# Output items of a fused attention and spectral kernel: the last 64 rows moved to the middle, the second half by batch

## The chip, the cores and the metric

The kernel runs on one core of one Trainium2 chip. Its time is the device time of one execution in microseconds (us); the median of several runs is the time of a kernel. A profile is of one execution, and gives the span from the first to the last thing that the profiler saw; the execution's own time is a little longer than its span.

## The reference

Eight batches, eight heads, 576 positions, head dimension 64. A sparse attention (heads 0 to 3 look back 31 positions, heads 4 to 7 look at earlier positions of the same residue modulo 32) gives `x` of 8 x 576 x 512. Then the lowest 64 Fourier modes along the positions are mixed by one complex 512 x 512 matrix each, transformed back to `y`, and the output is `u + relu(u @ w_ch)` with `u = x + y`:

```python
X = np.fft.rfft(x, axis=1)
Y[:, :n_modes] = Yr + 1j * Yi          # per mode: X[:, m] times (w_r[m] + i w_i[m])
y = np.fft.irfft(Y, n=S, axis=1)
u = x + y
return (u + np.maximum(u @ w_ch, 0.0)).astype(np.float32)
```

The output is 8 x 576 x 512 in float32, 9.4 MB. The weights `w_r` and `w_i` are 134 MB in float32, loaded once and converted to float16 on the way.

## The kernel before

Attention comes first, then the mixing of the modes, with the weight loads (issued by GpSimd, L182 to L190) running from the start to about 394 us. Beside the modes each batch is mixed ahead: `premix` leaves `v0s[b]` (x times w_ch) and `xos[b]` (x itself), each 128 partitions x 4 x 512 for the rows 0 to 511, and `v0h`, `xoh` for the last 64 rows of two batches together. `renew` adds to them what the first spectra give. The order of the instructions is written by hand: every engine runs its own in the order in which the program gives them.

What is left after the last weights is the **tail**, from L1044 on. The spectra of the last 16 modes are made (`spec_z` and the transposes of L1053) and kept as `zzs` (spectra times w_ch) and `yys` (spectra): `zzs[0]` and `yys[0]` hold batches 0 to 3, `zzs[1]` and `yys[1]` batches 4 to 7, in 32 partitions for each batch, so that batch b lies in partitions 32 * (b % 4) and up. `zzs[1]` is made later, from `spec_z(3, 1, held)` in the loop (L1068), while `yys[1]` is made with `yys[0]`.

The output is then made in 18 **items**, numbered k from 0 to LAST = 17. Each is 128 partitions x 2 x 512 float32, 512 KB. The rows of a batch are in five groups t: for t < 4, partition p of group t holds the row 256 * (t // 2) + 2p + t % 2, and t = 4 is the last 64 rows (512 to 575).

- Items 0 to 7 are the pairs of batches (0, 1) and (2, 3) in turn, for t = 0, 1, 2, 3; items 8 to 15 the pairs (4, 5) and (6, 7). Such an item goes out in one transfer on SP's queue (L1028), with rows of 2 KB in the output; item 0 in two pieces.
- Items 16 and 17 are t = 4 for batches 0 to 3 and 4 to 7. Partitions 0 to 63 hold the even batch of a pair, 64 to 127 the odd one. They go out in eight transfers of 64 partitions, 128 KB each (L1031): six on SP's queue, two on ScalarE's.

One item is made in these steps. `v_early(k)`: two matmuls with the identity put v0 into PSUM (L987). `new_rows(k, vps[k], zzs)`: two matmuls with 32 rows each add the last modes (L1001); those of a pair use two of the four groups of 32 rows of TensorE. `v_done(k)`: ScalarE's Relu (L1013) into `rl`. `u_early`, `new_rows(k, ups[k], yys)`: the same for u (L992, L1001). `u_done(k)`: VectorE adds PSUM and `rl` into `osb` (L1020), and SP issues the transfer. The loop over k (L1067) writes the v part of item k between the u parts of k - 1, so the matmuls of L1001 for two neighbouring items stand together: zz of item k, then yy of item k - 1. The pairs alternate so that these four use four different row groups.

`osb` has five buffers (tag "w" of the pool `pw`); `rl` has four; vps and ups turn over three PSUM tiles "p" and one "u".

Of the kernel before, what the change touches and what calls it, by code (L numbers as in the profile page):

```python
# [56 lines left out]
def kernel(  # L57
# [10 lines left out]
    nc = tc.nc  # L68
# [17 lines left out]
    def psum(kind, half=False, pair=False):  # L86
        if pair:
            return pss[kind].tile([128, 2, 512], FP, tag=kind, name=kind)
        if half:
            return pss[kind].tile([128, 1024], F16, tag=kind, name=kind)  # L90
        return pss[kind].tile([128, 512], FP, tag=kind, name=kind)
# [146 lines left out]
    def normalise(val, den, n, pieces, dst):  # L238
        rec = pin.tile([128, 8], FP, tag="rec", bufs=4, name="rec")
        nc.vector.reciprocal(out=rec[0:n, 0:pieces], in_=den)  # L240
        nc.vector.tensor_tensor(  # L241
            out=dst,
            in0=val.rearrange("p h (q c) -> p h c q", c=4),
            in1=rec[0:n, 0:pieces]
            .to_broadcast((n, pieces, 64))
            .rearrange("p h (q c) -> p h c q", c=4),
            op=AluOp.mult,
        )

    def act_copy(out, in_):  # L250
        nc.scalar.activation(out=out, in_=in_, func=ACTF.Copy)  # L251
# [445 lines left out]
    def out_cols(t):  # L697
        if t < 4:
            return ds(256 * (t % 2) + 128 * (t // 2), 128)
        return ds(512, 64)  # L700
# [32 lines left out]
    def spec_z(g, bq, zp):  # L733
        for e in range(4):
            lhs = YS["YT"][:, e, g, ds(8 * bq, 8), :].rearrange("p x m -> p (x m)")
            nc.tensor.matmul(
                zp, lhs, w_chs["n"][:, e, :], start=(e == 0), stop=(e == 3)
            )
# [130 lines left out]
    zzs = [ptr.tile([128, DM], F16, name=f"zz{i}") for i in range(B)]  # L869
    yys = [ptr.tile([128, DM], F16, name=f"yy{i}") for i in range(B)]  # L870
# [31 lines left out]
    A3 = cs["cFl"].rearrange("p a t m -> p (a t m)")[:, 0:S]  # L902
# [64 lines left out]
    for n, i in enumerate([3, 5, 7] + list(range(8, 21))):  # L967
        b, t = n // 2, n % 2 * 2
# [1 line left out]
        if n % 4 == 3:  # L970
            late.setdefault(i + (b == B - 1), []).append(lambda b=b: renew(b, (4,)))

    items = []
    for P0 in (0, 2):
        items += [((2 * P, 2 * P + 1), t) for t in range(4) for P in (P0, P0 + 1)]
    items += [(range(b, b + 4), 4) for b in (0, 4)]
    LAST = len(items) - 1
    vps, ups, rls, osbs = {}, {}, {}, {}

    def own(item, kept, half):  # L980
        bs, t = item
        return [kept[b][:, t] for b in bs] if t < 4 else [half[b // 2] for b in bs[::2]]

    def v_early(k):
        vps[k] = psum("p", pair=True)
        for j, r in enumerate(own(items[k], v0s, v0h)):
            nc.tensor.matmul(vps[k][:, j], idn, r, start=True, stop=False)  # L987

    def u_early(k):
        ups[k] = psum(("p", "u")[k % 2], pair=True)  # L990
        for j, r in enumerate(own(items[k], xos, xoh)):
            nc.tensor.matmul(ups[k][:, j], idn, r, start=True, stop=False)  # L992

    def new_rows(k, acc, spectra):
        bs, t = items[k]
        for j, b in enumerate(bs):
            q = ds(32 * (b % 4), 32)
            o, cols = acc[:, j % 2], out_cols(t)
            if t == 4:
                o = acc[ds(64 * (b % 2), 64), j // 2]  # L1000
            nc.tensor.matmul(  # L1001
                o, A3[q, cols], spectra[b // 4][q], start=False, stop=True
            )

    def pieces(k):
        return [slice(0, 1), slice(1, 2)] if k == 0 else [slice(0, 2)]

    def v_done(k):
        rl = ptr.tile([128, 2, 576], FP, tag=("xT", "rl")[k // 2 % 2], bufs=2, name="rl")
        rls[k] = rl[:, :, 0:DM]  # L1010
        vp = vps.pop(k)
        for j in pieces(k):
            nc.scalar.activation(out=rls[k][:, j], in_=vp[:, j], func=ACTF.Relu)  # L1013

    def u_done(k):
        bs, t = items[k]
        up, rl = ups.pop(k), rls.pop(k)
        osb = pw.tile([128, 2, DM], FP, tag="w", name="osb")
        for j in pieces(k):
            nc.vector.tensor_tensor(  # L1020
                out=osb[:, j], in0=up[:, j], in1=rl[:, j], op=AluOp.add
            )
            if t < 4:
                rows = out[:, ds(128 * (t - t % 2), 256), :].rearrange(
                    "b (p i) e -> p b i e", i=2
                )
                own_b = slice(bs[0] + j.start, bs[0] + j.stop)
                nc.sync.dma_start(rows[:, own_b, t % 2], osb[:, j])  # L1028
        if t == 4:
            for b in bs:  # L1030
                (nc.scalar if b % 2 and k == LAST else nc.sync).dma_start(  # L1031
                    out[b, ds(512, 64), :], osb[ds(64 * (b % 2), 64), b // 2 % 2, :]
                )

    flush()
# [9 lines left out]
    with tc.tile_pool(name="ps_s", bufs=1, space=PSUM) as pss["s"]:  # L1045
        zp = pss["s"].tile([128, 512], FP, name="zp")
        yp = pss["s"].tile([128, 2, 512], F16, name="yp")
        spec_z(3, 0, zp)
        act_copy(zzs[0], zp)
        for bq in range(2):  # L1050
            for e in range(4):
                lhs = YS["YT"][:, e, 3, ds(8 * bq, 8), :].rearrange("p x m -> p (x m)")
                nc.tensor.transpose(yp[:, bq, ds(128 * e, 128)], lhs, idn)  # L1053
        for bq in range(2):
            nc.vector.tensor_copy(out=yys[bq], in_=yp[:, bq])
    pss["u"] = pctx.enter_context(tc.tile_pool(name="ps_u", bufs=1, space=PSUM))

    for k in range(2):
        new_rows(k, vps[k], zzs)
    for k in range(2):  # L1060
        v_done(k)
    for k in range(2):
        if k:
            u_early(k)
        new_rows(k, ups[k], yys)
        u_done(k)
    for k in range(2, LAST + 2):  # L1067
        if k == 8:  # L1068
            held = psum("p", pair=True)[:, 0]
            spec_z(3, 1, held)  # L1070
            act_copy(zzs[1], held)
        if k <= LAST:
            v_early(k)
        if k > 2:
            u_early(k - 1)
        if k <= LAST:
            new_rows(k, vps[k], zzs)
        if k > 2:
            new_rows(k - 1, ups[k - 1], yys)
        if k <= LAST:  # L1080
            v_done(k)
        if k > 2:
            u_done(k - 1)
# [31 lines left out]
```

## Time and profile before

| what | value |
|---|---|
| median of 6 runs | 429.23 us (428.49 to 429.43) |
| the profiled execution's own time | 428.49 us |
| its span | 426.7 us |
| TensorE busy | 346.0 us (81%), 4167 matmuls |
| VectorE busy | 235.0 us (55%) |
| ScalarE busy | 218.5 us (51%) |
| GpSimd busy | 110.7 us (26%) |
| transfers issued by GpSimd (inputs, weights) | 81.28 MB, 96.3% of 16 engines' span |
| transfers issued by SP (output, two constants) | 9.39 MB, 6.1% |
| HBM read, written | 162.83 MB, 9.44 MB |

The transfers of item 0's two pieces are issued at 396.5 us, the last of all at 423.1 us. From issue to landing the 512 KB transfers take 3.4 us in the median and the 128 KB ones 2.5 to 2.6 us. In a row of the timeline stand start, length, engine, line, operation and its operands, and in brackets how long the engine had been idle and what released it. A share of the DMA is the mean busy share of the core's 16 DMA engines. A PE row covers several matmuls where it has a count, and their ends are modelled.

### The profile page before, as it was taken

The page shows a single profiled execution, that of the slowest core. Times are in us where ns is not written, and L with a number is a line of the kernel's source. Part 1 is how long each engine was busy: PE and PEld are TensorE (multiplying, and loading weights), DVE is VectorE, ACT ScalarE, POOL GpSimd, SP SyncE. Part 2 cuts the span into 40 slices and gives each one's busy share as a digit, 9 for nine tenths or more (in the row PEclk, how much of TensorE's full clock was granted, in tenths as well). Part 3 has the DMA queues.
Part 4 walks back from the last instruction along what each step waited for, and adds up shares of the span by engine and source line. Part 5 has one row for each costly group of instructions (what it writes and reads, how often), then busy time and mean ns, then how long its engine had stood idle before and what let it go on. Part 6 is the DMA issues. An engine that isn't in the chain of part 4 may idle for free.

```text
span 426.7 us, 9767 instructions
## 1 busy us (share of the span) xinstructions
PE 346.0 (81%) x4167; PEld 208.3 (49%) x4167; DVE 235.0 (55%) x466; ACT 218.5 (51%) x390; POOL 110.7 (26%) x196
## 2 busy tenths in 40 slices
PE   2987878779999698889676779876989868889993
PEld 2866767554656365556433444443444424435330
DVE  3788778851355154356203247755576363555883
ACT  1687778643656456565542325422452444434872
POOL 7433332322423222222221322232222222110000
PEclk9999899957999899999986889999899978979998
DMA  8999999999999999999999999999999999995698
GB/s 150 214 211 213 213 212 213 210 211 211 214 214 212 213 214 214 212 215 213 211 215 208 213 214 214 211 214 215 212 212 214 212 214 214 214 212 105 257 357 272
DMA packets 30938, 91.62 MB, mean 215 GB/s; under 512 B 4464, under 2 KB 5232, under 8 KB 30896
## 3 DMA queue, kind: packets, MB, share of 16 engines
q0 software_dynamic: 25168, 81.28, 96.3%
q1 hardware_dynamic: 5136, 9.39, 6.1%
q8 instruction: 32, 0.52, 0.5%
q10 hardware_dynamic: 592, 0.35, 0.3%
q14 instruction: 10, 0.08, 0.0%
HBM read 162.83 MB, written 9.44 MB: 404 GB/s over the span
## 4 chain that ended last, share of the span: by engine, by line
DMA 53%; PE 25%; DVE 12%; ACT 5%; issue 3%; POOL 1%; DVEq 0%; ACTq 0%; POOLq 0%
DMA wt<-in_moe_w_i_dram 43%; DMA wt<-in_moe_w_r_dram 4%; DMA ring<-in_v_dram 4%; PE y L597 4%; DVE xb L241 3%; PE p L987 2%; DVE kz L283 2%; PE sc L532 2%; ACT X L251 2%; PE p L760 2%; DMA ring<-in_q_dram 1%; PE p L1001 1%; DVE yy L752 1%; DVE rec L240 1%; PE sc L717 1%
## 5 line engine op out<-in xcount | busy, mean ns | idle before, releaser
L597 PE MATMUL y<-wt,X 128*32 128x512 f16 (+1 forms) x448 | 68.1, 415 | 22.6 <-DMA wt<-in_moe_w_i_dram 22.6
L186 POOL DMA_DIRECT2D wt<-in_moe_w_r_dram x59 | 34.6, 587 | 119.7 <-PE y L597 35.7
L186 POOL DMA_DIRECT2D wt<-in_moe_w_i_dram x60 | 35.4, 589 | 74.1 <-DMA wt<-in_moe_w_i_dram 50.7
L597 PEld LDWEIGHTS <-X 128*32 128x32 f16 (+1 forms) x448 | 27.7, 139 | 40.4 <-DMA wt<-in_moe_w_i_dram 21.6
L726 ACT ACTIVATE v<-sc 128x512 f16<-128x512 f32 x32 | 19.1, 597 | 47.9 <-PE sc L717 47.9
L727 DVE COPY xo<-tp 128x512 f16<-128x512 f16 x32 | 22.1, 692 | 38.5 <-PE tp L725 38.4
L717 PE MATMUL sc<-w_cp,xT 128*128 128x512 f16 x128 | 36.9, 411 | 1.4 <-DVE xT L690 1.4
L241 DVE TENSOR_TENSOR xb<-av,rec 90x256 f16<-90x256 f32 (+2 forms) x80 | 36.0, 450 | 2.8
L489 ACT ACTIVATE PL<-sc 128x480 f16<-128x480 f32 (+1 forms) x48 | 26.9, 578 | 20.3 <-PE sc L475 19.9
L240 DVE RECIPROCAL rec<-av 90x4 f32<-90x4 f32 (+2 forms) x80 | 14.6, 183 | 39.3 <-PE av L504 28.6
L251 ACT ACTIVATE yr<-y 128x512 f16<-128x512 f32 x28 | 16.7, 597 | 35.8 <-PE y L597 34.7
L961 DVE TENSOR_TENSOR xo<-p,xo 128x1024 f16<-128x1024 f32 x16 | 19.6, 1225 | 22.1 <-PE p L760 22.1
L420 DVE COPY qT<-tp 128x576 f16<-128x576 f16 x16 | 11.9, 752 | 32.3 <-PE tp L413 32.3
L251 ACT ACTIVATE v<-p 128x1024 f16<-128x1024 f32 x16 | 16.4, 1024 | 22.8 <-PE p L760 22.8
L378 ACT ACTIVATE PL<-sc 90x360 f16<-90x360 f32 (+1 forms) x48 | 22.8, 490 | 6.9 <-PE sc L371 6.4
L251 ACT ACTIVATE v<-tp 128x640 f16<-128x640 f16 (+1 forms) x24 | 19.0, 807 | 12.4 <-PE tp L447 9.0
L413 PE MATMUL tp<-cI_s,ring 64*64 64x64 f16 x864 | 22.8, 198 | 2.1 <-DVE qT L420 1.7
L459 PE MATMUL sc<-cMl_s,cI_s 128*128 128x480 f16 (+1 forms) x48 | 18.8, 391 | 5.3 <-ACT PL L489 3.7
L251 ACT ACTIVATE kz<-tp 64x360 f16<-64x360 f16 (+1 forms) x32 | 18.9, 592 | 6.1 <-PE tp L413 5.2
L276 PE MATMUL tp<-cI_s,ring 72*128 72x72 f16 x256 | 15.4, 207 | 8.2 <-DMA ring<-in_v_dram 6.6
L413 PEld LDWEIGHTS <-ring 64*64 64x64 f16 x864 | 18.0, 112 | 8.3 <-issue 4.2
L1013 ACT ACTIVATE rl<-p 128x1024 f32<-128x1024 f32 (+1 forms) x19 | 18.4, 979 | 5.7 <-PE p L1001 3.0
(142 smaller groups left out, 741.0 us busy)
## 6 DMA issues: line engine op xcount, KB each, us to landing
wt<-in_moe_w_i_dram POOLq DMA_DIRECT2D x60, 512.0 KB, 18.4
wt<-in_moe_w_r_dram POOLq DMA_DIRECT2D x59, 512.0 KB, 18.0
out_dram<-osb SPq DMA_DIRECT2D x15, 512.0 KB, 3.4
ring<-in_v_dram POOLq DMA_DIRECT2D x8, 288.0 KB, 13.2
ring<-in_q_dram POOLq DMA_DIRECT2D x8, 288.0 KB, 13.4
ring<-in_k_dram POOLq DMA_DIRECT2D x8, 288.0 KB, 13.1
ring<-in_v_dram POOLq DMA_DIRECT2D x3, 512.0 KB, 14.9
ring<-in_q_dram POOLq DMA_DIRECT2D x3, 512.0 KB, 14.8
```

The costliest lines, as they stand in the source:

```text
L186: nc.gpsimd.dma_start(dst, rows)
L240: nc.vector.reciprocal(out=rec[0:n, 0:pieces], in_=den)
L241: nc.vector.tensor_tensor(out=dst, in0=val.rearrange("p h (q c) -> p h c q", c=4), in1=rec[0:n, 0:pieces] .to_broadcast((n, pieces, 64)) . ...
L251: nc.scalar.activation(out=out, in_=in_, func=ACTF.Copy)
L378: nc.scalar.activation(out=PS[0:n, ds(POFF[t], 4 * n)], in_=scp[0:n, 0 : 4 * n], func=ACTF.Exp, scale=SCALE,)
L413: nc.tensor.transpose(tp[ds(64 * hp, 64), ds(64 * i, 64)], qn[ds(64 * hp, 64), ds(64 * (9 * g + i), 64)], idn[ds(64 * hp, 64), ds(64 * hp, ...
L489: nc.scalar.activation(out=dst, in_=src, func=ACTF.Exp, scale=SCALE)
L597: nc.tensor.matmul(yp[ds(a, 32), :], Xh[half][pr, c].rearrange("p b r (h m) -> p (b r h) m", h=2)[:, :, mm % 32], wt[pr, XC[c], :], start= ...
L717: nc.tensor.matmul(vp, xT[:, ch], w_chs["cp"][:, ch, :], start=(ch == 0), stop=(ch == 3),)
L726: nc.scalar.activation(out=v0, in_=vp, func=ACTF.Copy)
L727: nc.vector.tensor_copy(out=xo.rearrange("p (h q c) -> p h q c", h=2, c=4), in_=tp[:, 0:512].rearrange("p (h c q) -> p h q c", h=2, c=4),)
L961: nc.vector.tensor_tensor(out=xo, in0=up[:, 0:n], in1=xo, op=AluOp.add)
```

## The change

Four things change, all in the tail.

- The order of the items. Items 0 to 7 stay. The 64-row item of batches 0 to 3 becomes item 8, that of batches 4 to 7 item 13. The other eight, for batches 4 to 7, are made for one batch each instead of a pair: an item is (b, t) with t = 0 or 2, and its two halves are the groups t and t + 1. Since row 2p lies in group t and row 2p + 1 in group t + 1, a partition then holds two neighbouring rows, 4 KB without a break in the output. The order is (4, 0), (5, 0), (4, 2), (5, 2) as items 9 to 12 and the same for batches 6 and 7 as items 14 to 17.
- A swapped copy. `other` copies `spectra[1]` to `spectra[2]` with the partition halves exchanged, by two GpSimd copies of 64 x 512, for `yys` right after it is made and for `zzs` after `zzs[1]`. The two matmuls of a batch in `new_rows` read one of each, so they use the row groups b % 4 and (b + 2) % 4, and the neighbour's use the other two.
- The transfers. A 64-row item goes out in two transfers of 64 partitions x 2 batches, 256 KB each, both on SP's queue; ScalarE issues none. A batch's item goes out in one with 4 KB rows; the last item is computed and sent in two pieces, as item 0 is, with 2 KB rows.
- `spec_z(3, 1, held)` and its copy to `zzs[1]` stand before item 6 in the loop instead of before item 8.

The number of matmuls, adds and Relus is the same but for the last item's pieces; SP issues 21 output transfers where SP and ScalarE issued 25.

```diff
-    items = []
-    for P0 in (0, 2):
-        items += [((2 * P, 2 * P + 1), t) for t in range(4) for P in (P0, P0 + 1)]
-    items += [(range(b, b + 4), 4) for b in (0, 4)]
+    items = [((2 * P, 2 * P + 1), t) for t in range(4) for P in (0, 1)]
+    items += [((b,), t) for b0 in (4, 6) for t in (0, 2) for b in (b0, b0 + 1)]
+    items.insert(8, (range(0, 4), 4))
+    items.insert(13, (range(4, 8), 4))
...
     def own(item, kept, half):
         bs, t = item
+        if len(bs) == 1:
+            return [kept[bs[0]][:, t], kept[bs[0]][:, t + 1]]
         return [kept[b][:, t] for b in bs] if t < 4 else [half[b // 2] for b in bs[::2]]
+
+    def other(spectra):
+        for a in (0, 64):
+            nc.gpsimd.tensor_copy(out=spectra[2][ds(64 - a, 64)], in_=spectra[1][ds(a, 64)])
...
     def new_rows(k, acc, spectra):
         bs, t = items[k]
+        if len(bs) == 1:
+            for j, src in ((0, spectra[1]), (1, spectra[2])):
+                q = ds(32 * ((bs[0] + 2 * j) % 4), 32)
+                nc.tensor.matmul(
+                    acc[:, j], A3[q, out_cols(t + j)], src[q], start=False, stop=True
+                )
+            return
...
     def pieces(k):
-        return [slice(0, 1), slice(1, 2)] if k == 0 else [slice(0, 2)]
+        return [slice(0, 1), slice(1, 2)] if k in (0, LAST) else [slice(0, 2)]
...
-                nc.sync.dma_start(rows[:, own_b, t % 2], osb[:, j])
+                to = rows[:, own_b, t % 2] if len(bs) > 1 else rows[:, bs[0], j]
+                nc.sync.dma_start(to, osb[:, j])
         if t == 4:
-            for b in bs:
-                (nc.scalar if b % 2 and k == LAST else nc.sync).dma_start(
-                    out[b, ds(512, 64), :], osb[ds(64 * (b % 2), 64), b // 2 % 2, :]
+            for b in bs[0:2]:
+                nc.sync.dma_start(
+                    out[b : bs[-1] + 1 : 2, ds(512, 64), :].rearrange("j p e -> p j e"),
+                    osb[ds(64 * (b % 2), 64)],
                 )
...
         for bq in range(2):
             nc.vector.tensor_copy(out=yys[bq], in_=yp[:, bq])
+        other(yys)
...
-        if k == 8:
+        if k == 6:
             held = psum("p", pair=True)[:, 0]
             spec_z(3, 1, held)
             act_copy(zzs[1], held)
+            other(zzs)
```

## The prediction

> **What bounds the kernel now.** I read the page's table of slices first, then the windows of the last 30 us, then their timeline. From 20 us on, for some 370 us, the loads of weights and inputs fill the DMA engines; nothing there is touched. What the change touches begins at 396.5 us, where the first output transfer is issued. The two lines of the page show the share of time in which the DMA engines were busy and the bytes moved:
>
> ```profile
> DMA  8999999999999999999999999999999999995698
> GB/s 150 214 211 213 213 212 213 210 211 211 214 214 212 213 214 214 212 215 213 211 215 208 213 214 214 211 214 215 212 212 214 212 214 214 214 212 105 257 357 272
> ```
>
> The last slice is full by its digit (8), yet moves 272 GB/s where the slice before moves 357. The windows split that stretch (window, its length, busy time and count of each engine, PEclk, DMA share, GB/s):
>
> ```profile
> 397.40:399.00 1.60, 1.60 (x11) 0.58 (x10) 1.32 (x2) 1.28 (x2) 0.00 (x0) 1.00 0.83 309
> 399.00:400.50 1.50, 1.50 (x11) 0.43 (x9) 1.43 (x2) 1.23 (x2) 0.00 (x0) 1.00 0.78 288
> 400.50:407.50 7.00, 6.86 (x43) 2.20 (x42) 5.55 (x5) 5.04 (x6) 0.00 (x0) 1.00 1.00 374
> 407.50:408.50 1.00, 1.00 (x8) 0.33 (x8) 0.93 (x2) 0.97 (x1) 0.00 (x0) 1.00 0.37 133
> 408.50:420.90 12.40, 10.80 (x72) 3.24 (x68) 11.28 (x10) 8.24 (x9) 0.00 (x0) 1.00 1.02 379
> 420.90:422.20 1.30, 0.00 (x0) 0.00 (x0) 0.00 (x0) 0.00 (x0) 0.00 (x0) 1.00 0.92 211
> 422.20:422.90 0.70, 0.00 (x0) 0.00 (x0) 0.00 (x0) 0.00 (x0) 0.00 (x0) 0.91 0.94 190
> 422.90:423.50 0.60, 0.00 (x0) 0.00 (x0) 0.00 (x0) 0.00 (x0) 0.00 (x0) 0.50 1.03 383
> 423.50:425.20 1.70, 0.00 (x0) 0.00 (x0) 0.00 (x0) 0.00 (x0) 0.00 (x0) 0.50 0.86 252
> ```
>
> An item is 512 KB of output (524 kB). At 374 to 379 GB/s it takes the DMA 1.40 to 1.38 us. It is supplied faster than that, as the timeline of VectorE's adds shows (start, length):
>
> ```profile
> 402.57 1.23 DVE L1020 TENSOR_TENSOR osb<-u,rl 128x1024 f32<-128x1024 f32 x1
> 403.87 1.23 DVE L1020 TENSOR_TENSOR osb<-p,rl 128x1024 f32<-128x1024 f32 x1
> 406.33 1.23 DVE L1020 TENSOR_TENSOR osb<-u,rl 128x1024 f32<-128x1024 f32 x1 [1.24 <-PE u L1001]
> 407.63 1.23 DVE L1020 TENSOR_TENSOR osb<-p,rl 128x1024 f32<-128x1024 f32 x1
> ...
> 415.21 0.60 PE L987 MATMUL p<-v0h,cI_s 128*128 128x512 f16 x2
> ...
> 416.83 0.61 PE L987 MATMUL p<-v0h,cI_s 128*128 128x512 f16 x2
> ...
> 419.68 1.21 DVE L1020 TENSOR_TENSOR osb<-u,rl 128x1024 f32<-128x1024 f32 x1
> 419.79 3.94 SPq L1031 DMA_DIRECT2D out_dram<-osb  x6
> ```
>
> One add comes every 1.30 us, so the stream of writes falls 0.1 us further behind with each item, and the stream sets the end. It loses time in three places: before it is full (until 400.5), at 407.5 to 408.5 (a share of 0.37, so 0.63 us idle) and from 420.9 to 425.2, where the two items of the last 64 rows go out in eight transfers of 64 partitions. While SP's queue alone feeds them the rate is 211 GB/s, with the engines busy. Computing ends at 420.9; the rest is writing.
>
> **The change, part by part.** The sum is of the profiled execution: its span is 426.7 us, its own time 428.49, so 1.8 lie outside the span; it is the fastest of the six runs, 0.74 below their median of 429.23. I add the change of the span to the median.
>
> *The 64-row items, from places 16 and 17 to 8 and 13.* Each is now two transfers of 256 KB (262 kB), partitions 0 to 63 and then 64 to 127, both in SP's queue. At 211 GB/s one takes 1.24 us, an item 2.48, both 4.97. They took 425.2 - 420.9 = 4.3. So +0.67. Bounds: if the two halves ran side by side, an item would take 1.38 as a whole one does, both 2.76: -1.54; above, at the 190 of the slowest window, 5.52: +1.2. I take 211, because that window has one queue alone, as the new kernel will; the 383 stands where ScalarE's queue held transfers of the other half as well, and the change takes that queue away. Moving the items hides nothing by itself: the stream has no idle time there to put them in.
>
> The Trainium skill speaks against this edit (DMA: Bandwidth & Descriptors, Rules for kernel authors): transfers of the two partition halves gain nothing from being two, from one issuing engine or from two, since they serialise, and one transfer of 128 partitions is to be used. The 211 agrees with that and the 383 does not. By the rule this part stays at +0.67; by the 383 it would be near the lower bound.
>
> On TensorE such an item costs more than others: from L987 at 415.21 to the next at 416.83 are 1.62 us, not 1.30, because its four matmuls of 64 columns use all four row groups, and those of its neighbour can't run beside them. It meets a neighbour twice, so there are four such slots, 0.3 each, where there were two (1.2 in all, 0.65 more). Items 13 and 14 meet it with the stream well behind (item 8's slow writes), so that costs nothing; without that cover it is 0.6. At items 7 and 8 the stream is behind by only 0.1 to 0.2, so I count +0.3 (0 to +0.6).
>
> *The late spectrum (spec_z, its copy) from before item 8 to before item 6.* Its matmuls put the adds back by 2.46 - 1.30 = 1.17 us (403.87 to 406.33), of which the stream shows 0.63 as idle; what it was behind hid the rest. Two items earlier it is 0.2 less behind: +0.2 (0 to +0.5).
>
> *4 KB rows in the second half.* Eight items go by batch, so a partition writes one row of 4 KB; seven keep it whole, the last is cut into two transfers with 2 KB rows. A 2 KB row takes 16 x 2048 / 379 = 86.5 ns of an engine. No longer row of output is in the trace. In the 211 window a row takes 155 ns, and if two engines share one path there, a path passes a row in 77.6 (71.5, with the share of 0.92), so 9 to 15 ns belong to the row, not its bytes. A row of 4 KB then takes 164 to 158 ns, an item of 8 rounds 1.31 to 1.265. The weights' 8 KB rows in DRAM say nearly the same (the page's lines of queues and of HBM): 162.83 MB in 96.3% of 426.7 us, 396 GB/s, 1.32. I take 1.29: 7 x (1.38 - 1.29) = -0.65. Bounds: -0.85, and no gain at all; a loss I hold to +0.2, since neither longer row is slower.
>
> *GpSimd's copies, four of 64x512.* The nearest is L329, 128x576, 1.17 us, so 1.04 each; between 0.5 (half the partitions) and 2.3 (partitions are crossed, which no row shows). The pair for zzs starts when ScalarE has copied: 1.67 us after the matmuls (403.67 to 405.34), now from 401.1, so at 402.8, and ends at 404.9. It is first read at item 9's L1001, at 407.10 + 0.32 = 407.4. Even at 2.3 each it ends at 407.4. Behind that wait stand TensorE's later matmuls and so the stream, which item 8 occupies about 1 us longer than item 9 needs to arrive. The pair for yys runs from 395.2 to 397.4 and is read after 408: nothing. It runs beside the first adds (395.78). VectorE's vT copy beside L329 took 0.61 us, as its eight runs do (0.59 to 0.61), so I count 0; were the adds to wait for the copies they would be 1.6 late, and with 0.6 idle before the stream is full that is +1.0. GpSimd's DMA queue has issued its last load before.
>
> *What is left.* The swapped copies let a batch's two matmuls use row groups that its neighbour leaves free, so the pace stays 1.30. If that failed, eight items at 1.62 would end the adds at some 424, still ahead of a stream that ends at 425.7. The last item's add in two pieces (2 x 0.69, for 1.21) ends near 421.6, four us ahead of the stream: nothing. SP's two issues of 0.5 to 0.8 per 64-row item stand before item 9's, hidden by the 2.48 us of writing. ScalarE's two issues go: nothing.
>
> Sum: 0.67 + 0.3 + 0.2 - 0.65 = +0.5. The span becomes 427.2, the median 429.7.
>
> **The rivals.** *A, the halves overlap.* The engines drift apart, some read the upper half while others are in the lower, and an item takes 1.38. For: 383 GB/s at 422.9. Against: 420.9 to 422.2 holds a lower and then an upper half in one queue, at 211 throughout. Time: -1.54 + 0.3 + 0.2 - 0.65 = -1.7: 427.5, faster.
>
> *B, slower: the long rows bring nothing.* Place: items 9 to 16. If writing to DRAM, not the row, limits the 379, an item stays at 1.38 and the -0.65 falls away: +1.2, 430.4. It decides from 1.34 us an item on, where the sum passes +0.86. For: 379 holds over 12.4 us without a break, like a limit. Against: the 8 KB rows' 396.
>
> *C, the copies hold up the first adds:* +0.5 + 1.0, 430.7. For: no row has GpSimd beside an add of this form. Against: the vT copy beside L329.
>
> *D, it doesn't do what it says* (no row groups beside each other): by the above no more than the forecast, so no case of its own.
>
> **How the numbers follow.** The measurement can tell 0.2%, 0.86 us, from no change. Forecast: 0.60, its own range -0.2 to +1.2 (429.0 to 430.4) by the bounds of rows and halves; 0.46 of it within 0.2%, 0.12 above, 0.02 below. A 0.20 and 0.02 for a faster stream by some other way: faster. B 0.13, C 0.05: slower. Together faster 0.24, same 0.46, slower 0.30. The range is from A's time, with about half of A below it, to just above B: 427.5 to 430.7.
>
> **What would show it.** The share of the DMA near 1 from item 8's transfers to the end; about 210 GB/s for 2.5 us twice, at some 410 and 418 us; 395 to 410 GB/s between and after; adds over by 421.6, data until 425.7; two copies on GpSimd near 403, done before 407. Wrong if the rate stays near 380 in the 64-row items (A), is 380 with 4 KB rows (B), if L1020 starts after 396 (C), or if TensorE waits for GpSimd at item 9.

## The result, and the profile after

The changed kernel takes 429.84 us (median of 23 runs, 429.04 to 431.67) beside 428.85 for the kernel before (49 runs, 427.30 to 430.35). The medians differ by 0.99 us. The ratio over all runs, in which the eight slowest of the 23 count (430.6 to 431.7), is 1.0033, with a 95% interval of 1.0024 to 1.0043: 1.4 us slower, by 1.0 to 1.8. The profiled execution has a span of 428.0 us (before: 426.7). SP issues 22 output transfers in it, not the 21 that were counted ahead.

These are the two lines of the page's table of slices:

```profile
DMA  8999999999999999999999999999999999994797
GB/s 151 213 213 212 213 213 212 211 211 212 214 214 212 214 214 213 213 214 214 211 214 211 214 215 213 209 214 214 212 205 215 213 214 213 214 213 85 285 324 275
```

The last slice has the rate of before (275 for 272), though the half transfers have left it; the slice ahead of it, where one of them now stands, moves 324 for 357. The windows of the changed kernel, cut where its stream of writes changes pace, show why (window, length, busy time and count of PE, PEld, DVE, ACT and POOL, PEclk, DMA share, GB/s). Its first output transfer is issued at 396.14, 0.36 us earlier in the span than before:

```profile
396.14:404.70 8.56, 8.42 (x49) 2.69 (x48) 6.71 (x7) 6.44 (x8) 1.37 (x3) 1.00 0.82 303
404.70:405.50 0.80, 0.80 (x8) 0.26 (x6) 0.80 (x1) 0.80 (x1) 0.00 (x0) 1.00 0.12 44
405.50:409.80 4.30, 4.30 (x29) 1.38 (x28) 3.42 (x4) 2.82 (x4) 0.00 (x0) 1.00 0.98 365
409.80:410.35 0.55, 0.55 (x7) 0.13 (x6) 0.55 (x1) 0.35 (x1) 0.00 (x0) 1.00 0.05 15
410.35:412.90 2.55, 2.55 (x20) 0.80 (x16) 2.41 (x3) 2.05 (x2) 0.00 (x0) 1.00 0.93 217
412.90:417.80 4.90, 4.90 (x34) 1.64 (x31) 3.95 (x5) 3.30 (x4) 0.00 (x0) 1.00 1.01 395
417.80:420.40 2.60, 1.95 (x12) 0.48 (x9) 2.53 (x3) 1.88 (x3) 0.00 (x0) 1.00 0.95 288
420.40:423.70 3.30, 0.00 (x0) 0.00 (x0) 0.99 (x2) 0.00 (x0) 0.00 (x0) 1.00 1.01 402
423.70:425.20 1.50, 0.00 (x0) 0.00 (x0) 0.00 (x0) 0.00 (x0) 0.00 (x0) 0.76 0.98 380
425.20:426.50 1.30, 0.00 (x0) 0.00 (x0) 0.00 (x0) 0.00 (x0) 0.00 (x0) 0.50 0.22 85
```

Row by row, after the first: the late spectrum leaves 0.70 us of 0.80 idle (before: 0.63); another 0.52 is idle just ahead of the first 64-row item; that item is written at 217 GB/s, which is 2.42 us for its 524 kB (the window also holds the first 30 kB of the next); the items with 4 KB rows go at 395 to 402 GB/s, where the 2 KB rows went at 379; the second 64-row item is written between its neighbours, 749 kB at 288 together. All of that is close to the forecast. The last row is not: from 425.2 to 426.5 the share is 0.22, so a few of the 16 engines are still writing while the others are done. In the kernel before the last 0.8 us of data had a share of 0.44 and then none:

```profile
424.70:425.50 0.80, 0.00 (x0) 0.00 (x0) 0.00 (x0) 0.00 (x0) 0.00 (x0) 0.50 0.44 131
425.50:426.30 0.80, 0.00 (x0) 0.00 (x0) 0.00 (x0) 0.00 (x0) 0.00 (x0) 0.50 0.00 0
```

The trace has 16 landings for each transfer, one by each DMA engine. Counted from the first issue of each profiled execution (which moves between 395.7 and 397.8 us of the span from one to the next, so the ends of spans compare badly), each entry is the first of the 16 landings + the width, which is how much later the last one came; for each 64-row item its first and its last transfer are given:

```
                     64-row transfers in the middle              last transfer   last landing
before               none                                        28.8 + 0.4      29.18
after                16.1+0.2  16.7+1.3 | 22.8+1.1  23.4+2.2     29.0 + 1.6      30.65
x1_end               none                                        29.0 + 0.3      29.26
x2_pairs             16.1+0.2  16.8+1.3 | 23.0+1.4  24.4+1.0     30.0 + 0.5      30.51
x3_two_queues        16.1+0.2  16.7+1.5 | 23.6+0.7  24.2+1.8     29.6 + 1.3      30.99
x4_full              15.8+0.2           | 23.0 + 0.2             28.3 + 0.2      28.44
y1_both_early         9.7+0.3  10.4+0.6 | 17.6+0.3  18.3+1.2     28.6 + 1.1      29.70
y2_first_early        9.7+0.3  10.4+0.6 | 23.1+0.2  23.7+1.3     28.8 + 1.2      30.02
y3_no_swap           16.2+0.2  16.9+1.3 | 23.9+0.8  24.5+1.5     29.9 + 1.2      31.01
y4_one_end            9.7+0.2  10.4+0.6                          28.0 + 0.3      28.36
z1_four_small        15.2+0.2 to 17.1+0.3 | 22.6+0.7 to 24.3+0.7 29.6 + 0.3      29.93
z2_one_end_pairs      9.7+0.2  10.3+0.7                          28.9 + 0.6      29.45
z3_low_low           15.1+0.2 to 17.0+0.3 | 22.6+0.6 to 24.1+0.7 29.5 + 0.4      29.92
z4_one_end_pieces     9.8+0.2  10.5+0.6                          28.3 + 0.6      28.86
```

In the changed kernel the lower half of item 8 lands within 0.2 us, the upper half over 1.3, and every later transfer stays 1.1 to 1.3 wide until item 13 makes it 2.2. At the end the first engine is done 1.6 us ahead of the last; 0.54 of that is the last engine alone. The changed kernel's last landing is 1.47 us later than that of the kernel before. The runs with small transfers at the same places (z1, z3) end 0.7 later than that kernel, so about half of the 1.47 goes with the form of the transfers.

### The profile page after: what moved, and what is told of

The parts are those of the page before. It is cut to its first block, busy times and chain, and to the rows that moved or that the text cites. A ratio compares the mean times of both kernels' runs of the same rounds, so it can differ in the third digit from the quotient of the medians.

```text
span 428.0 us, 9772 instructions
## 1 busy us (share of the span) xinstructions
PE 342.3 (80%) x4167; PEld 206.9 (48%) x4167; DVE 235.0 (55%) x467; ACT 218.4 (51%) x391; POOL 113.2 (26%) x200
## 4 chain that ended last, share of the span: by engine, by line
DMA 56%; PE 14%; DVE 5%; ACT 2%; issue 2%; DVEq 0%; POOL 0%; ACTq 0%
DMA wt<-in_moe_w_i_dram 45%; DMA wt<-in_moe_w_r_dram 6%; DMA ring<-in_v_dram 4%; PE y L597 3%; PE p L993 2%; PE sc L717 1%; DVE yy L752 1%; DVE osb L1033 1%; PE p L1014 1%; PE p L998 1%; ACT X L251 1%; PE y L532 1%; PE u L998 1%; PE sc L459 1%; DVE xb L241 1%
## 5 line engine op out<-in xcount | busy, mean ns | idle before, releaser
L717 PE MATMUL sc<-w_cp,xT 128*128 128x512 f16 x128 | 35.8, 400 | 1.9 <-DVE xT L690 1.9
```

The costliest lines, as they stand in the source:

```text
L717: nc.tensor.matmul(vp, xT[:, ch], w_chs["cp"][:, ch, :], start=(ch == 0), stop=(ch == 3),)
```

## The experiments

Each kernel is the changed one with one edit; ratios are against the kernel before, with 95% intervals.

**x1_end: the order undone.**

```diff
-    items.insert(8, (range(0, 4), 4))
-    items.insert(13, (range(4, 8), 4))
+    items += [(range(b, b + 4), 4) for b in (0, 4)]
...
```

with the eight transfers at the end as before, and only item 0 in two pieces.

> The changed kernel with the order undone: the two 64-row items are items 16 and 17 again and go out in eight transfers as before the change (six on SP's queue, two on ScalarE's); the by-batch items with 4 KB rows, the swapped copies and the early spec_z stay; only item 0 is cut in two. Theory 1, drift: in the changed kernel the 64-row transfers do not only cost their bytes at 211 GB/s, they also set the 16 DMA engines apart (one item's landing spreads over 1.3 us where it was 0.3), the engines never meet again, and the last engine ends about 1 us after the mean; then undoing the order takes away 0.67 + 0.3 for the slow writes and the slots, and about 1.0 for the drift, and the eight 4 KB items keep their gain: about -0.5 against the kernel before, ratio 0.9985 to 0.9995. Theory 2, issue: it is SP that is late, since its issues of 4 KB rows took 0.6 to 1.3 us where 2 KB rows took 0.37; then the loss stays: ratio 1.002 to 1.004. Theory 3, long rows cost elsewhere: also 1.002 or more.

428.84 us, ratio 1.0005 (0.9993 to 1.0016). The loss goes with the order, so theories 2 and 3 fall: SP issued the 4 KB transfers in 0.33 us here, and its 0.6 to 1.3 us in the changed kernel are those of an issue into a queue that is behind. But the gain of the long rows did not come either. The middle of this run has the fast stream (the same windows view, at a by-batch item):

```profile
410.06:412.61 2.55, 2.55 (x17) 0.80 (x16) 2.40 (x3) 2.00 (x3) 0.00 (x0) 1.00 1.00 402
```

402 GB/s is 1.30 us for an item, which is just the pace of supply. The last add ends 24.6 us after the first issue (24.4 before), the eight small transfers follow it, and the last landing is at 29.26 (29.18 before). In the kernel before the first landing of items 14 and 15 came 3.2 and 3.0 us after their issue, for 2.5 and 2.4 here, so its stream was 0.6 us behind its supply; but the first small transfer, held up by a slower slot on TensorE, landed 2.0 to 2.1 us after its issue in both, so faster rows had next to nothing to win.

**x2_pairs: the rows undone.**

```diff
-    items += [((b,), t) for b0 in (4, 6) for t in (0, 2) for b in (b0, b0 + 1)]
+    items += [((2 * P, 2 * P + 1), t) for t in range(4) for P in (2, 3)]
...
```

and no swapped copies.

> The changed kernel with the rows undone: items of batches 4 to 7 are pairs with 2 KB rows again and the swapped copies are gone; the 64-row items stay in the middle (8 and 13) with two transfers each on SP's queue, the early spec_z and the last item's two pieces stay. Theory 1 (drift): all of the loss stays and the gain of 4 KB rows, 0.7, is lost as well: +2.1 against before, ratio 1.0045 to 1.0055. Theory 2 (issue of 4 KB rows is the loss): SP is quick again, ratio 1.000 to 1.002.

430.64 us, ratio 1.0049 (1.0030 to 1.0067). The loss is not in the long rows: it stays without them. Whether it is larger (1.0049 for 1.0033) is not shown, since the intervals overlap.

**x3_two_queues: the upper half from ScalarE.**

```diff
-                nc.sync.dma_start(
+                (nc.scalar if b % 2 else nc.sync).dma_start(
```

> The changed kernel with the upper half of each 64-row item issued by ScalarE instead of SP, nothing else. Theory 1: the halves are read side by side, a 64-row item takes 1.4 to 1.8 us instead of 2.5 and the engines stay together: -2 to -3 against the changed kernel, ratio 0.996 to 0.999 against before. The page's rule that halves serialise from one queue or two: no change, ratio 1.002 to 1.004. ScalarE's wait for the add and 0.6 us of issue may put one Relu back by 0.3 us.

430.97 us, ratio 1.0051 (1.0032 to 1.0071). Theory 1 missed here: both halves were issued within 0.01 us, and the window that starts 14.2 us after the first issue, as long as the changed kernel's for item 8, moved no more than its 217 GB/s:

```profile
409.87:412.42 2.55, 1.87 (x15) 0.76 (x12) 1.67 (x3) 1.97 (x3) 0.00 (x0) 1.00 0.93 215
```

The halves of one item do serialise, from two queues as from one, as the Trainium skill has it (DMA: Bandwidth & Descriptors, Rules for kernel authors). The view of queues (packets, MB, share of the 16 engines) has SP's queue q1 alone at 410.3 to 411.2, at 187 GB/s, and ScalarE's queue q10 nearly alone at 411.4 to 412.0, at 290:

```profile
q1 hardware_dynamic: 82, 0.17, 97.7%
q10 hardware_dynamic: 84, 0.17, 98.8%
```

The 383 GB/s in the kernel before, which spoke for rival A, was no overlap either. The same view at 422.9 to 423.3 and at 423.3 to 423.5 of that run:

```profile
DMA packets 92, 0.15 MB, mean 364 GB/s; under 512 B 21, under 2 KB 21, under 8 KB 92
q1 hardware_dynamic: 69, 0.13, 86.0%
DMA packets 52, 0.08 MB, mean 420 GB/s; under 512 B 11, under 2 KB 11, under 8 KB 52
q10 hardware_dynamic: 41, 0.08, 107.6%
```

One queue wrote and then the other, each at the full rate by itself. So a transfer of 64 partitions is not slow in itself. Its 2 KB rows took 84 ns each in the median there, and 151 ns from 420.9 on, in the window of 211 GB/s. Why some of these transfers are slow and others not is open. ScalarE paid for the issue: the last add ended 26.3 us after the first issue, for 25.3.

**x4_full: what the halves cost.** Each 64-row item goes out in one transfer of 128 partitions, four pieces of 1 KB each; the last 64 rows of the batches then hold the data in another order, so the output is not the reference's, while the bytes, the items' places and the computing stay.

```diff
-            for b in bs[0:2]:
-                nc.sync.dma_start(
-                    out[b : bs[-1] + 1 : 2, ds(512, 64), :].rearrange("j p e -> p j e"),
-                    osb[ds(64 * (b % 2), 64)],
-                )
+            nc.sync.dma_start(
+                out[bs[0] : bs[-1] + 1, ds(512, 64), :].rearrange("b r (h e) -> (r h) b e", h=2),
+                osb.rearrange("p j (x e) -> p (j x) e", x=2),
+            )
```

> The changed kernel with each 64-row item sent in one transfer of 128 partitions with four 1 KB pieces a partition; the 64 rows of a batch then hold its items' halves in another order, the bytes and the place of the item are the same. It measures what the halves cost. Theory 1: with all 128 partitions the stream runs at 340 to 380 GB/s through the item and the engines stay together: 2 us or more less than the changed kernel, ratio 0.996 to 0.998 against before. Theory 2: ratio stays at 1.002 to 1.004, since the issue of 4 KB rows is as it was.

428.97 us, ratio 1.0000 (0.9988 to 1.0013). The window of item 8 in it:

```profile
411.99:414.54 2.55, 2.55 (x20) 0.83 (x16) 2.41 (x3) 2.05 (x2) 0.00 (x0) 1.00 1.04 384
```

384 for 217 GB/s, landings 0.2 us wide to the end, and the loss is gone. It is 1.4 us, not the 2 or more that were expected: with the halves gone the stream catches up with its supply, which four slow slots and the late spectrum hold up all the same.

**y1_both_early and y2_first_early: other places.**

```diff
-    items.insert(8, (range(0, 4), 4))
-    items.insert(13, (range(4, 8), 4))
+    items.insert(4, (range(0, 4), 4))
+    items.insert(9, (range(4, 8), 4))      # in y2_first_early: 13
```

> The changed kernel with the two 64-row items at other places: that of batches 0 to 3 is item 4, so its slow writes go out while the late spectrum holds up the adds, and that of batches 4 to 7 is item 9, ahead of all by-batch items. Theory 1 (drift): the first item's slow writes fill the 0.85 us in which the stream stood idle at the late spectrum, the engines meet again there, and eight items of 4 KB rows, which take 1.27 us and are supplied every 1.30, give the engines time to meet after the second: 1 to 2 us less than the changed kernel, ratio 0.999 to 1.0013 against before. Rival, the bytes alone: only the idle time is won, 0.85, ratio 1.001 to 1.002. Rival, place does not matter: 1.003.

429.14 us, ratio 1.0009 (0.9996 to 1.0022).

> The changed kernel with the 64-row item of batches 0 to 3 as item 4, that of batches 4 to 7 at 13 as it was. Theory 1 (drift): the idle 0.85 us is filled, but the second item sets the engines apart shortly before the end, so the last landing still spreads over 0.8 us or more: ratio 1.0005 to 1.002. If the spread of the end came from the first item alone, the spread falls under 0.4 us and the ratio is that of the kernel with both early.

429.79 us, ratio 1.0019 (1.0003 to 1.0035). Both are as theory 1 had them, though the intervals are as wide as the steps between its rivals. The table of landings says more than the time: an item at place 4 is followed by the stall of the late spectrum, and the next transfer lands within 0.4 us; an item at 9 or 13 leaves 1.1 to 1.2 us to the end (the changed kernel's two: 1.6). The expectation for y1, that eight items of 4 KB rows would bring the engines together, missed: they landed 1.1 to 1.3 us wide throughout, in a stream that never waited.

**y3_no_swap: both matmuls read the same partitions.**

```diff
-            for j, src in ((0, spectra[1]), (1, spectra[2])):
-                q = ds(32 * ((bs[0] + 2 * j) % 4), 32)
+            for j, src in ((0, spectra[1]), (1, spectra[1])):
+                q = ds(32 * (bs[0] % 4), 32)
...
```

and no copies by GpSimd.

> The changed kernel without the swapped copies: both matmuls of a batch read the same 32 partitions of the plain copy, GpSimd copies nothing. The prediction says that TensorE then takes 0.3 us more for each of the eight by-batch items, 2.4 in all, and that this is hidden, since the adds end some 4 us ahead of the stream: ratio 1.0025 to 1.0045, as the changed kernel. Rival: the adds become the bound, ratio 1.005 or more. If the copies themselves had cost something, the ratio falls below 1.0025.

430.92 us, ratio 1.0045 (1.0031 to 1.0059). Its adds, from the timeline:

```profile
418.72 1.22 DVE L1033 TENSOR_TENSOR osb<-p,rl 128x1024 f32<-128x1024 f32 x1 [0.30 <-PE p L1005]
420.23 1.22 DVE L1033 TENSOR_TENSOR osb<-u,rl 128x1024 f32<-128x1024 f32 x1 [0.29 <-PE u L1005]
421.74 1.22 DVE L1033 TENSOR_TENSOR osb<-p,rl 128x1024 f32<-128x1024 f32 x1 [0.28 <-PE p L1005]
```

They come every 1.51 us and wait 0.3 for TensorE; in the changed kernel the same stretch reads

```profile
416.38 1.23 DVE L1033 TENSOR_TENSOR osb<-p,rl 128x1024 f32<-128x1024 f32 x1
417.67 1.23 DVE L1033 TENSOR_TENSOR osb<-u,rl 128x1024 f32<-128x1024 f32 x1
418.97 1.23 DVE L1033 TENSOR_TENSOR osb<-p,rl 128x1024 f32<-128x1024 f32 x1
```

1.30 and no wait. So the swapped copies do what they say, worth 1.9 us of supply (last add at 27.2 for 25.3 after the first issue), and of that the last landing shows 0.36 (31.01 for 30.65): the stream, late for another reason, hides the rest. The medians differ by more, 1.1 us, but the intervals of the two ratios overlap. The result lies at the edge of its range.

**y4_one_end and z2_one_end_pairs: one 64-row item early, one last.** The first is item 4; the last goes out in four transfers of 64 partitions, two on each queue. z2 has pairs with 2 KB rows besides.

```diff
-    items.insert(8, (range(0, 4), 4))
-    items.insert(13, (range(4, 8), 4))
+    items.insert(4, (range(0, 4), 4))
+    items.append((range(4, 8), 4))
...
```

> The changed kernel with the 64-row item of batches 0 to 3 as item 4 (two transfers on SP's queue) and that of batches 4 to 7 last, in four transfers of 64 partitions, two on SP's queue and two on ScalarE's; only item 0 is cut in two. Half of the slow writes are then behind the late spectrum and half stay at the end. Theory 1: against the order undone (1.0005) the end loses about 2 us of slow writes, the middle gains at most 1: ratio 0.9965 to 0.999. Rival: the stream carries the first item's slow writes on to the end, so nothing is won: 1.000 to 1.001.

428.38 us, ratio 0.9994 (0.9982 to 1.0006).

> The kernel with one 64-row item early (item 4, two transfers) and one last (four transfers on two queues), with pairs and 2 KB rows in the second half and no swapped copies. If the 4 KB rows matter once the stream is the bound, this is 0.5 to 0.9 us slower than the same with 4 KB rows (0.9994): ratio 1.0005 to 1.0015. Rival: the stream is ahead of the supply there, as in the order undone, and the rows bring nothing: ratio 0.9985 to 1.0003.

429.48 us, ratio 1.0018 (1.0005 to 1.0032). In y4 the stream is full from the late spectrum to the last item:

```profile
402.50:404.50 2.00, 2.00 (x15) 0.57 (x14) 1.16 (x1) 1.18 (x2) 1.22 (x2) 1.00 0.66 189
404.50:421.00 16.50, 14.39 (x90) 4.37 (x88) 14.67 (x13) 11.26 (x11) 0.00 (x0) 1.00 1.02 385
```

The slow half writes stand where the adds are held up, and the stream carries nothing on. Between the two runs only the rows and what goes with them differ: 0.0024 of the time, 1.0 us, with intervals that overlap from 1.0005 to 1.0006; the last landings differ by 1.1 us (29.45 and 28.36). So long rows pay where the stream is what ends last.

**z1_four_small and z3_low_low: what sets the engines apart.** The 64-row items stay at 8 and 13 and go out in four transfers of 128 KB, one a batch, all on SP's queue; z1 in the order of the batches (low, high, low, high), z3 as low, low, high, high.

```diff
-            for b in bs[0:2]:
-                nc.sync.dma_start(
-                    out[b : bs[-1] + 1 : 2, ds(512, 64), :].rearrange("j p e -> p j e"),
-                    osb[ds(64 * (b % 2), 64)],
-                )
+            for b in bs:                       # in z3_low_low: (*bs[::2], *bs[1::2])
+                nc.sync.dma_start(
+                    out[b, ds(512, 64), :], osb[ds(64 * (b % 2), 64), b // 2 % 2, :]
+                )
```

> The changed kernel with each 64-row item sent as four transfers of 64 partitions and 128 KB, one per batch, all on SP's queue, at the same places 8 and 13. Theory 1a, the shape sets the engines apart: the eight small transfers at the end of the kernel before left landings 0.1 to 0.4 us wide, while each pair of 256 KB transfers, two rows a partition, left them 1.3 us wide; so the spread stays under 0.5 us here, the slow writes stay, and the end comes about 1 us earlier than in the changed kernel: ratio 1.000 to 1.0015. Theory 1b, any slow half in a busy stream sets them apart: spread 1 us or more at the end, ratio 1.0025 to 1.0045. SP's four issues of 0.6 us put item 9's transfer back by 1.2 us, which the slow writes hide.

429.85 us, ratio 1.0025 (1.0013 to 1.0037).

> The changed kernel with each 64-row item sent as four transfers of 128 KB on SP's queue, in the order low, low, high, high (batches 0, 2, 1, 3), where the run with four small transfers alternated low and high and left its last landing 0.3 us wide (29.6 to 29.9 us after the first issue; the changed kernel 29.0 to 30.65). It separates the length of a run on one half from the two rows a partition in one transfer. If a long run on one half sets the engines apart: spread 1 us or more at the end, last landing 30.3 to 30.7 after the first issue, ratio 1.0025 to 1.0045. If the two-row transfer does: spread under 0.6, last landing 29.8 to 30.1, ratio 1.0015 to 1.0035.

429.77 us, ratio 1.0021 (1.0006 to 1.0036). The end of the changed kernel's stream, and the same times after the first issue (28.2, 29.0 and 29.8) in z1, in the windows view:

```profile
424.34:425.14 0.80, 0.00 (x0) 0.00 (x0) 0.00 (x0) 0.00 (x0) 0.00 (x0) 0.58 0.97 374
425.14:425.94 0.80, 0.00 (x0) 0.00 (x0) 0.00 (x0) 0.00 (x0) 0.00 (x0) 0.50 0.39 149
425.94:426.74 0.80, 0.00 (x0) 0.00 (x0) 0.00 (x0) 0.00 (x0) 0.00 (x0) 0.50 0.04 15
```

```profile
425.41:426.21 0.80, 0.00 (x0) 0.00 (x0) 0.00 (x0) 0.00 (x0) 0.00 (x0) 0.50 1.03 394
426.21:427.01 0.80, 0.00 (x0) 0.00 (x0) 0.00 (x0) 0.00 (x0) 0.00 (x0) 0.50 0.48 179
427.01:427.81 0.80, 0.00 (x0) 0.00 (x0) 0.00 (x0) 0.00 (x0) 0.00 (x0) 0.50 0.00 0
```

z1 wrote its two 64-row items no faster (200 GB/s where item 8 has 217) and has no fewer bytes left at 28.2 (458 kB for 430), but it stops within its second window, where the changed kernel trails on into its third. Both runs of small transfers end at 29.9 with a width of 0.3 to 0.4, so it is the transfer of 256 KB with two rows a partition that sets the engines apart, not a long run on one half; whether its size or its second row does it was not tried. In the traces, one for each run, this is 0.7 us of the end (30.65 to 29.9). The times point the same way (1.0025 and 1.0021 for 1.0033), but their intervals overlap, so the times alone do not show it.

**z4_one_end_pieces: y4 with the last add in two pieces** and the first two small transfers issued after the first.

```diff
+            elif k == LAST:
+                for b in bs[2 * j.start : 2 * j.start + 2]:
+                    (nc.scalar if b % 2 else nc.sync).dma_start(
+                        out[b, ds(512, 64), :], osb[ds(64 * (b % 2), 64), j.start, :]
+                    )
...
```

> The kernel with one 64-row item early (item 4) and one last, 4 KB rows and swapped copies, with the last item's add in two pieces and its first two transfers issued after the first piece. In the run without the pieces (0.9994) the last items landed 2.3 to 2.7 us after their issue, as in an idle queue, so the supply sets its end there: the first two small transfers leave 0.55 us earlier and the end follows by 0.3 to 0.5: ratio 0.998 to 0.9994, last landing 27.8 to 28.1 after the first issue (28.36 without). If the slow writes of the last item set the end whatever their start: 28.3 and 0.9988 to 1.0.

428.74 us, ratio 0.9999 (0.9984 to 1.0014), last landing 28.86 (y4: 28.36): nothing won, against the expectation. No version here is faster than the kernel before by more than its interval; y4 comes nearest.

## Why the prediction was right or wrong

The time of 429.84 lies in the range and 0.14 from the point, but the point leaned on a median of before that later runs put 0.4 lower, so that nearness is luck. What counts is the difference: +0.5 was forecast and +1.4 measured, so "within 0.2%", the likeliest case, is not what happened; a small loss is. By the steps:

- *The 64-row items.* Forecast 2.48 us each; 2.42 for item 8 at the rate of its window. Item 13 has no window of its own: if its neighbours' 225 kB went at 395 GB/s, some 2.0 us are left for it, an estimate. So the cost was near the forecast, and "moving the items hides nothing by itself" holds: no run with the halves at 8 and 13 beats the kernel before. What the 383 GB/s were was misread: they were one queue at a time, not two halves side by side. And the bound from above, 190 GB/s for 211, was put around the rate alone.
- *The slots on TensorE, and the late spectrum.* Idle time of the stream 0.70 + 0.52 = 1.22 us for a forecast of 0.83 + 0.3. Right.
- *4 KB rows.* 1.29 us an item forecast, 1.30 to 1.33 measured. Right, and rival B falls with it.
- *GpSimd.* Two copies took 1.26 us together, not 2.1; the first add followed 0.55 us after VectorE was free, as before. Rival C falls:

```profile
395.03 1.26 POOL L988 COPY yy<-yy 64x512 f16<-64x512 f16 x2 [12.68 <-DVE yy L1070]
395.42 1.29 DVE L1033 TENSOR_TENSOR osb<-p,rl 128x512 f32<-128x512 f32 x2 [0.55 <-ACT rl L1026]
402.45 1.28 POOL L988 COPY zz<-zz 64x512 f16<-64x512 f16 x2 [6.16 <-ACT zz L251]
```

- *What is left.* That a failing swap would be hidden: mostly, by the traces (0.36 of 1.9 us at the end).
- *The end of the stream* is the step that failed. The prediction ended it at 425.7 us, as if 16 engines were one server; with the first issue 0.36 earlier that is 425.3, and the stream does run at 380 GB/s to 425.2. Then it took 1.3 us more. The term that was put at nothing is the width between engines, about 0.7 us by the traces of z1 and z3; with it the forecast is +1.2, inside the measured 1.0 to 1.8. That the loss comes with the half transfers is shown by the times of x1 and x4; this split of it is from traces alone.
- *Rival A* was judged by the right row (211) and given 0.20 by the wrong one: the drift that was to help the stream is what delayed its end. Its price was too high as well: where the halves are gone (x4) the time is that of the kernel before, not 1.7 us less, since the supply then sets the pace.

## What to carry to other kernels

A slow transfer moved into the middle of a full stream is not hidden there (the changed kernel, z1 and z3 are all slower); it was hidden where the stream waits anyway, as behind the late spectrum in y4. Before a fast window is read as two transfers side by side, see which queue wrote in it. A queue over 16 engines ends with its slowest engine, so read the first and the last landing of a transfer and not only the rate. Longer rows pay where the stream is behind its supply (1.0 us between y4 and z2) and nothing where it is level (x1).

## What the runs showed of the hardware

Two 256 KB transfers of 64 partitions, two 2 KB rows each, one half after the other in a full queue, land 0.2 and 1.3 us wide (item 8); the same bytes as four 128 KB transfers land 0.2 to 0.3 wide. The 16 landings of the upper half are spread over the 1.3 us, and the engines stay apart while the queue is never empty: the 1.3 us after item 8 of the changed kernel were still 1.2 four transfers later.

Not every spread comes from the halves. In the kernel before, at item 0's second piece, 15 engines land within 0.2 us and one lands 2.4 later. At that time, 399.0 to 400.5, the view of queues has one packet of an instruction load, 16 KB that occupied one engine for 0.93 us:

```profile
q8 instruction: 1, 0.02, 3.9%
```

That this packet held the engine up is not shown; every run has such a packet there and a late engine after it. The late one was still 0.9 us behind the other 15 after six more transfers, and the stall at the late spectrum ended it: landings 1.1 us wide became 0.3 where the stream was idle for 0.63 us (407.5 to 408.5), and 1.1 became 0.2 where it was idle for 0.70 in the changed kernel.

Which engines fall behind, and why the upper half and not the lower, the trace does not tell, and it was not tried. Two queues did not make the halves of an item overlap (215 GB/s for 217), and a 64-partition transfer went at 211 GB/s in one window and at 364 to 420 in others.
